# The first batch's attention cut into three query tiles, each followed by its LayerNorm and first MLP layer

## The chip, the cores and the metric

The kernel runs on one core of one Trainium2 chip. The metric is the device time of one execution in microseconds (us), from launch to the end of the last output write. The engines are TensorE (PE, matmuls; PEld are its weight loads), VectorE (DVE), ScalarE (ACT), GpSimd (POOL) and SyncE (SP), which here only starts DMAs. Each engine works through its own instructions in order and waits on semaphores for the others; ACT and POOL start some DMAs too.

## The reference

Eight batches of 12 heads, 448 tokens of 64 elements in each head; the heads' outputs side by side (768 columns) go through a LayerNorm and a two-layer MLP with 3072 hidden columns. All in float32 on input and output.

```
q_n = q / sqrt(mean(q*q) + 1e-6) * g_q ; k_n likewise with g_k       # over a head's 64 elements
P   = softmax(q_n @ k_n.T / 8) ; x = P @ v                           # [8, 12, 448, 64] -> [8, 448, 768]
xn  = (x - mean(x)) / sqrt(var(x) + 1e-6) * g_ln
out = x + relu(xn @ w_ch1) @ w_ch2                                   # w_ch1 [768, 3072], w_ch2 [3072, 768]
```

## The kernel before, in words

**Units.** Heads are taken in pairs, six pairs a batch, numbered p = 0 to 47 through all batches. A pair's 448 tokens lie as three full tiles of 128 and a left-over of 64 for each of the two heads, seven groups in all. Preparation works on units of two pairs (the first two units of batch 0 hold one pair each): squares on ACT (L218), sums on DVE (L221), a logarithm and an exponential on ACT for the inverse root (L224, L225), the keys times the product of the two gain vectors (L235, DVE or POOL), a high half of the keys in fp16 (L241 POOL or L243 ACT) and the remainder as a low half (L246, DVE), queries scaled and written twice (L68, L285). The keys' inverse root is not applied to the keys: it is the per-row scale of the exponential.

**Attention of a pair.** Seven key groups in turn: scores S (L359, a 128 x 448 matmul; the left-over groups L365 or L369 and L370), the exponential E (L377, ACT, 448 columns), and the product with v (V, L414 for three query tiles and L416 for the left-over, with a column of ones in v for the sum). L429 to L436 on DVE divide by the sums and write x. Keys and queries are transposed on PE through PSUM (L319, L322, L333, L336, copied out at L324, L339 and L341) up to unit 7, and by DMA transposes afterwards (L264 to L277).

**Order of the work.** For batch 0 the list ORDER gives, word by word, the program order of every step: letters a to m are preparation steps of a unit, K and Q transposes, S, V, T (LayerNorm statistics), A, N, X, R (the LayerNorm), U (`up_first`, the first 3 of 24 chunks of the first MLP layer), W0 to W2 (the weight loads of the first layer, 1024 columns each, issued on POOL) and L4 to L7 (unit loads, issued on SP). Every engine's queue follows this order. After it, `run_rest` interleaves two lists for each batch b: the MLP's chunks of batch b, and the attention steps of batch b+1, seven for each pair. `upto` keeps the steps in proportion to the chunks' costs, so that the steps are through when `tail` = 13 chunks of 960 cost units are left; then come the LayerNorm of batch b+1, four DMA transposes of its result on SP (L630), and these 13 chunks of the second layer (L674, psC) on PE beside it. The first layer's chunk is L658 (psH), six matmuls of 384 columns for an even batch (three token tiles) and 512 for an odd one, which also carries the left-over tokens of both; ACT applies the ReLU (L660).

**First loads.** `load_first` splits batch 0 over the ACT, SP and POOL queues pair by pair; SP's list ends with v. The second layer's weights (`load_w2`, two halves of 2304 KB) are started from the attention steps of units 6 and 7.

Of the kernel before, what the change touches and what calls it, by code (L numbers as in the profile page):

```python
# [32 lines left out]
z0 b2 a2 S0.2 d2 c2 S0.3 S0.4 K1 V0.0 e2 i2 S0.5 Q1 g2 l2 S0.6 S1.0 j2 V0.1 S1.1 S1.2 m2 b3  # L38
V0.2 a3 V0.3 k2 c3 S1.3 K2 V0.4 S1.4 z2 V0.5 Q2 S1.5 V0.6 V1.0 i3 W0 d3 e3 S1.6 V1.1 V1.2 S2.0
j3 T0 V1.3 S2.1 S2.2 Q3 V1.4 S2.3 K3 S2.4 V1.5 V1.6 S2.5 g3 z3 S2.6 V2.0 S3.0 S3.1 V2.1 k3  # L40
S3.2 b4 S3.3 V2.2 l3 a4 V2.3 m3 S3.4 V2.4 K4 S3.5 Q4 V2.5 V2.6 S3.6 Q5 S4.0 V3.0 S4.1 V3.1 i4
V3.2 d4 T1 K5 V3.3 W1 c4 V3.4 V3.5 S4.2 S4.3 V3.6 S4.4 S4.5 W2 e4 V4.0 V4.1 j4 S4.6 S5.0 k4
S5.1 g4 V4.2 l4 S5.2 V4.3 V4.4 V4.5 S5.3 K6 V4.6 z4 V5.0 S5.4 m4 b5 V5.1 G2 S5.5 L6 V5.2 S5.6
V5.3 V5.4 V5.5 Q6 a5 i5 V5.6 T3 T4 S6.0 S6.1 S6.2 S6.3 T5 S6.4 A V6.0 V6.1 N0 V6.2 N1 V6.3
S6.5 S6.6 d5 V6.4 X0 X1 U0 N2 R Q7 X2 c5 e5 j5 g5 k5 l5 z5 U1 U2 V6.5 M m5 V6.6 L7 K7
# [5 lines left out]
UP_FIRST = 3  # L51
# [25 lines left out]
class _Fast:  # L77


    def __init__(self, ctx, tc, sh, q, k, v, gs, g_ln, w1, w2, out):  # L80
# [57 lines left out]
    def load_first(self):  # L138
        nc = self.nc
        flat = self.hT.rearrange("p f n -> p (f n)").bitcast(FP32)  # L140
        t = [flat[:, 2688 * n:2688 * n + 2688].rearrange("p (w g d) -> p w g d", w=NPAIR, d=D)
             for n in range(2)]
        flat = self.sh.w2.rearrange("p f n -> p (f n)").bitcast(FP32)
        t.append(flat[:, 128:128 + 2688].rearrange("p (w g d) -> p w g d", w=NPAIR, d=D))
        main = lambda eng, n, p: self.load_main(eng, n, t[n][:, p, 0:6], 0, 2 * p, 2)
        left = lambda eng, n, p=0, m=NPAIR: self.load_left(eng, n, t[n][:, p:p + m, 6], 0, 2 * p, 2 * m)
        main(nc.scalar, 1, 0)
        left(nc.scalar, 1, 0, 1)
        main(nc.sync, 0, 0)
        left(nc.gpsimd, 0, 0, 1)  # L150
        main(nc.scalar, 0, 1)
        for n in range(2):
            nc.sync.dma_start(self.sh.gg[:, n], self.gs[n].unsqueeze(0))
        left(nc.gpsimd, 1, 1, NPAIR - 1)
        main(nc.sync, 1, 1)
        left(nc.sync, 0, 1, NPAIR - 1)
        for n, p in ((1, 2), (1, 3), (0, 2), (0, 3), (2, 0), (2, 1)):
            main(nc.sync, n, p)
        left(nc.sync, 2)
        for n, p in ((1, 4), (1, 5), (0, 4), (0, 5)):  # L160
            main(nc.sync, n, p)
        for p in range(2, NPAIR):
            main(nc.sync, 2, p)
        self.v_first = t[2]
        for u, (b, hs, m) in enumerate(UNITS):
            if b == 0:
                self.loads[u] = [x[:, hs // 2:hs // 2 + m].rearrange("p w g d -> p (w g) d")
                                 for x in t]
# [11 lines left out]
    def group(self, p, i):  # L180

        u, w = PAIR_UNIT[p]
        if UNITS[u][0] == 0:
            return 7 * w + i
        return 6 * w + i if i < 6 else 6 * UNITS[u][2] + w
# [6 lines left out]
    def pieces(self, u):  # L192
# [19 lines left out]
        def square(n):  # L212

            o = c["khl" if n == 1 else "qn"].rearrange("p g e d -> p (g e d)").bitcast(FP32)
            if u == 0 and n == 1:
                o = self.hT.rearrange("p f n -> p (f n)").bitcast(FP32)[:, 5376:5376 + g * D]
# [11 lines left out]
        def kg():  # L228
            if u == 0:
                nc.vector.tensor_tensor(out=sh.gprod[0:1], in0=sh.gg[:, 0], in1=sh.gg[:, 1],  # L230
                                        op=ALU.mult)
                ps = self.ps_m.tile([128, D], FP32, tag="mlp", name="psG")
                nc.tensor.matmul(ps, sh.row, sh.gprod[0:1], start=True, stop=True)
                nc.vector.tensor_copy(out=sh.gprod, in_=ps)
            (nc.vector if u in DVE_KG else nc.gpsimd).tensor_tensor(  # L235
                out=c["t"][1], in0=c["t"][1],
                in1=sh.gprod.unsqueeze(1).broadcast_to([128, g, D]), op=ALU.mult)
# [62 lines left out]

        def vall():

            nonlocal v16, vl, p1
            v16, vl, p1 = self.v16[:, 0:2], self.vl[:, 0:2], 2
            vmain()
            vleft()
# [4 lines left out]
                    z=vall if u == 0 else lambda: (vmain(), vleft()))  # L311


    def trans_k(self, p):
        nc, sh = self.nc, self.sh
        u, w = PAIR_UNIT[p]
        qn, khl = self.units[u][0:2]
        kT, ps = self.kU[PE_SET][:, 960 * (p % 2):960 * (p % 2) + 960], self.tr
        nc.tensor.matmul(ps[:, 0:256].rearrange("p (e o) -> p e o", e=2)[:, :, 0:D],  # L319
                         khl[:, self.group(p, 6)], sh.id16, is_transpose=True, start=True, stop=False)  # L320
        for i in range(6):
            nc.tensor.matmul(ps[:, 192 + 128 * i:320 + 128 * i], khl[:, self.group(p, i)], sh.id16,  # L322
                             is_transpose=True, start=False, stop=(i == 5))
        nc.vector.tensor_copy(out=kT, in_=ps[:, 0:960])  # L324

    def trans_q(self, p):
        nc, sh = self.nc, self.sh
        u, w = PAIR_UNIT[p]
        qn, khl = self.units[u][0:2]
        tr = self.ps_m.tile([128, 1024], FP16, tag="mlp", name="psQ") if p < NPAIR else self.tr  # L330
        ps = tr[:, 128:128 + 2 * S].rearrange("p (e s) -> p e s", e=2)
        qT = self.qU[PE_SET][:, p % 2].rearrange("p e s -> p (e s)")
# [5 lines left out]
        if p in ACT_Q:  # L338
            nc.scalar.copy(out=qT, in_=ps.rearrange("p e s -> p (e s)"))  # L339
# [106 lines left out]
    def first_attention(self):  # L446
# [531 lines left out]
```

## Time and profile before

| what | us |
|---|---|
| median of three runs | 603.84 (603.78 to 603.84) |
| span of the profiled execution, first to last instruction | 603.0 |
| PE busy | 577.6 |
| ACT busy | 358.5 |
| DVE busy | 287.8 |
| POOL busy | 184.8 |
| first exponential starts (timeline of ACT) | 12.08 |
| first 512-column first-layer matmul of batch 1 starts (timeline of PE) | 123.02 |

The profiled execution's span is 603.0 us; what lies around it up to the measured time of 603.84 us is 0.84 us, taken as fixed. A timeline row gives the start, the length, the engine, the line, what is written and read, the shape and how many instructions are merged; behind it, in brackets, stand the idle time before it and who ended it. A row of the stages' table gives, for a stretch of time, each engine's busy time with its instructions in brackets, then the granted TensorE clock, the busy share of the 16 DMA engines, and GB/s. Matmuls are pipelined: the length of one is longer than the distance to the next.

### The profile page before, as it was taken

How to read it: one execution, taken by the hardware profiler on the slowest of the kernel's cores; microseconds unless marked ns; L12 is line 12 of the kernel's file. 1: busy time of each engine (PE TensorE's matmuls, PEld its weight loads, DVE VectorE, ACT ScalarE, POOL GpSimd, SP SyncE). 2: the span in 40 equal slices, each digit the busy share in tenths (PEclk: the TensorE clock that was granted, in tenths of full speed). 3: DMA queues.
4: the chain of work that ended last, by engine and by line, in shares of the span. 5: the costliest groups of instructions: out<-in, count | busy, mean ns of one | idle time of the engine just before them, and what ended most of it. 6: DMA issues, size and time to landing. Idle time of an engine off the chain costs nothing.

```text
span 603.0 us, 11494 instructions
## 1 busy us (share of the span) xinstructions
PE 577.6 (96%) x4502; PEld 341.9 (57%) x4502; DVE 287.8 (48%) x645; ACT 358.5 (59%) x673; POOL 184.8 (31%) x246
## 2 busy tenths in 40 slices
PE   2877999999999999999999999999999999999997
PEld 1555566654566666655566666655556666654565
DVE  5798567734256255724256255642355422450011
ACT  5996887359743598548755498537765287114300
POOL 3844432232642345423542245505322000000000
PEclk9899999999999999999999999999999999999999
DMA  7999999574957578947866386848533330040011
GB/s 209 281 196 206 207 222 197 106 212 86 146 130 125 106 126 155 170 121 122 120 127 131 104 125 153 165 120 152 114 68 88 92 62 1 27 106 1 1 53 54
DMA packets 130285, 75.18 MB, mean 125 GB/s; under 512 B 96500, under 2 KB 120420, under 8 KB 130228
## 3 DMA queue, kind: packets, MB, share of 16 engines
q1 hardware_dynamic: 113092, 44.50, 37.7%
q0 software_dynamic: 16192, 29.30, 22.9%
q8 instruction: 36, 0.59, 0.4%
q10 hardware_dynamic: 944, 0.62, 0.3%
q14 instruction: 21, 0.17, 0.1%
HBM read 52.30 MB, written 11.01 MB: 105 GB/s over the span
## 4 chain that ended last, share of the span: by engine, by line
PE 88%; ACT 2%; DVE 2%; issue 0%; DVEq 0%
PE psC L674 36%; PE psH L658 35%; PE psS L359 8%; PE oA L414 5%; PE oB L416 2%; PE psS L365 1%; ACT E L377 1%; PE tr L322 0%; ACT khl L218 0%; PE psU L704 0%; DVE stat L582 0%; ACT hT L660 0%; PE tr L336 0%; DVE xn L603 0%; DVE x L431 0%
## 5 line engine op out<-in xcount | busy, mean ns | idle before, releaser
L658 PE MATMUL psH<-xnT,w 128*128 128x512 f16 (+1 forms) x1134 | 242.1, 353 | 0.0
L674 PE MATMUL psC<-w,hT 128*128 128x384 f16 (+1 forms) x1368 | 234.8, 324 | 0.0
L377 ACT ACTIVATE E<-psS,rr_all 128x448 f16<-128x448 f32 x312 | 193.5, 635 | 49.5 <-PE psS L359 48.6
L660 ACT ACTIVATE hT<-psH 128x512 f16<-128x512 f32 (+1 forms) x189 | 104.0, 550 | 130.9 <-PE psH L658 128.8
L674 PEld LDWEIGHTS <-hT 128*128 128x128 f16 x1368 | 127.2, 98 | 78.8 <-issue 4.3
L658 PEld LDWEIGHTS <-w 128*128 128x128 f16 x1134 | 102.3, 98 | 83.3 <-issue 2.9
L359 PE MATMUL psS<-qU,kU 128*128 128x448 f16 x288 | 101.3, 358 | 8.7 <-ACT E L377 5.8
L414 PEld LDWEIGHTS <-E 128*128 128x128 f16 x936 | 65.0, 99 | 44.3 <-issue 5.0
L235 POOL TENSOR_TENSOR qkv<-qkv,gprod 128x896 f32<-128x896 f32 x21 | 43.7, 2079 | 95.8 <-issue 51.7
L414 PE MATMUL oA<-v,E 128*128 128x65 f16 x864 | 66.9, 194 | 0.1
L678 DVE SCALAR_TENSOR_TENSOR x<-psC,rs_all,x 128x384 f32<-128x384 f32 x48 | 29.2, 616 | 78.4 <-PE psC L674 77.9
L128 POOL DMA_DIRECT2D qkv<-in_k_dram x14 | 11.1, 793 | 137.0 <-ACT E L377 64.3
L416 PE MATMUL oB<-v,E 128*128 128x65 f16 x288 | 52.1, 194 | 0.1
L429 DVE RECIPROCAL rec_all<-oA 128x6 f32<-128x6 f32 x48 | 9.3, 194 | 88.2 <-PE oA L414 87.8
L221 DVE TENSOR_REDUCE ssq<-khl 128x14 f32<-128x896 f32 (+1 forms) x24 | 25.6, 1065 | 44.6 <-ACT khl L218 44.5
L359 PEld LDWEIGHTS <-kU 128*128 128x128 f16 x288 | 28.2, 99 | 25.9 <-issue 6.0
L221 DVE TENSOR_REDUCE ssq<-qn 128x14 f32<-128x896 f32 (+1 forms) x25 | 26.2, 1046 | 21.8 <-ACT qn L218 21.7
L68 DVE SCALAR_TENSOR_TENSOR qn<-qkv,rr_all 128x256 f16<-128x256 f32 (+1 forms) x72 | 26.4, 426 | 18.1 <-ACT rr_all L225 18.1
L416 PEld LDWEIGHTS <-E 128*128 128x128 f16 x312 | 30.3, 97 | 0.2 <-DVE xl L436 0.2
L431 DVE TENSOR_TENSOR x<-oA,rec_all 128x384 f32<-128x384 f32 x48 | 26.8, 558 | 1.5
L582 DVE BATCH_NORM_STATS2 stat<-x 128x6 f32<-128x256 f32 (+1 forms) x75 | 26.0, 404 | 0.6
L246 DVE TENSOR_TENSOR khl<-qkv,khl 128x896 f16<-128x896 f32 x21 | 22.7, 1079 | 4.0 <-ACT khl L243 3.9
(114 smaller groups left out, 447.3 us busy)
## 6 DMA issues: line engine op xcount, KB each, us to landing
out_dram<-x SPq DMA_DIRECT2D x20, 384.0 KB, 2.5
qkv<-in_v_dram POOLq DMA_DIRECT2D x15, 384.0 KB, 6.5
qkv<-in_k_dram POOLq DMA_DIRECT2D x14, 384.0 KB, 3.9
qkv<-in_q_dram POOLq DMA_DIRECT2D x14, 384.0 KB, 5.4
w<-in_moe_w_ch_dram POOLq DMA_DIRECT2D x3, 1536.0 KB, 13.0
w<-in_moe_w_ch_dram POOLq DMA_DIRECT2D x2, 2304.0 KB, 24.8
qkv<-in_k_dram SPq DMA_DIRECT2D x7, 384.0 KB, 5.7
qkv<-in_q_dram SPq DMA_DIRECT2D x7, 384.0 KB, 6.0
```

What stands on the lines that cost most here:

```text
L68: nc.vector.scalar_tensor_tensor(out=out, in0=x, scalar=8.0, in1=r.unsqueeze(2).broadcast_to([x.shape[0], g, D]), op0=ALU.mult, op1=ALU.mult)
L221: nc.vector.tensor_reduce(out=c["ssq"][:, n], in_=c["sq", n], axis=AX.X, op=ALU.add)
L235: (nc.vector if u in DVE_KG else nc.gpsimd).tensor_tensor(out=c["t"][1], in0=c["t"][1], in1=sh.gprod.unsqueeze(1).broadcast_to([128, g, D] ...
L359: nc.tensor.matmul(ps[0][:, 0:S], c["main"][:, ts(i, 128)], c["q"][:, ts(h, S)], start=True, stop=True)
L377: nc.scalar.activation(out=o, in_=x[:, 0:S], func=AFT.Exp, scale=self.units[u][3][:, g:g + 1], bias=EXP_BIAS)
L414: nc.tensor.matmul(oA[:, t, cs], E[:, ts(t, 128)], rhs, start=(i == 0 and t == 0), stop=(i == 6 and t == 2))
L416: nc.tensor.matmul(oB[:, cs], E[:, 320:448], rhs, start=(i == 0), stop=(i == 6))
L431: nc.vector.tensor_tensor(out=x[:, :, 128 * hp:128 * hp + 128].rearrange("p t (e d) -> p t e d", e=2), in0=oA[:, :, :, 0:D], in1=rec[:, 0: ...
L658: nc.tensor.matmul(ps[:, 0:N], sh.w1[:, dc, ts(f, 128)], xnT[:, dc, 0:N], start=(dc == 0), stop=(dc == NDC - 1))
L660: nc.scalar.activation(out=hT[:, f, 0:N], in_=ps[:, 0:N], func=AFT.Relu)
L674: nc.tensor.matmul(ps[:, 0:g[1]], hT[:, f, ts(t, 128)], sh.w2[:, f, cols], start=(f == 0), stop=(f == NFF - 1))
L678: nc.vector.scalar_tensor_tensor(out=x[:, cols], in0=ps[:, 0:g[1]], scalar=self.rs[:, b, t:t + 1], in1=x[:, cols], op0=ALU.mult, op1=ALU.add)
```

## The change

Only batch 0 and the way into batch 1 change.

- Batch 0 runs in three phases: token tile 0, token tile 1, and token tile 2 with the left-over tokens. In each phase every pair's scores are taken for that phase's queries alone: 8 matmuls of 128 columns (phases 0 and 1), 9 pieces of 192, 128 or 64 columns (phase 2). The exponentials cover several key groups in one PSUM bank: 512 and 384 columns, in phase 2 512, 448 and 384.
- To allow this the keys are multiplied by their own inverse root in fp32 (L461) before they are split into halves, and the scale of the exponential is the constant 0.125. The gain vectors go into the queries, on POOL (L504). All six pairs' turned keys stay in SBUF.
- After each phase come that tile's division, LayerNorm (A, N, X, XC) and, for tiles 0 and 1, all 24 first-layer chunks in six groups of four (U, L641: 24 matmuls of 128 columns into one bank; R, L646: a ReLU of 512 columns). They stand between the scores of phases 1 and 2. Tile 2's six groups come from `mlp_chunks`, after ORDER.
- Loads: q and v of batch 0 go into the two buffers of the input ring, keys stay where they were. SP's list is reordered and ends with the left-over rows of q (`self.load_left(nc.sync, 0, ...)`, 196 KB in rows of 256 bytes). W0 stands in the order after the gain product of the second query part (qG0.2), W1 after z2 and j2, W2 after qG2.0; W3 and W4, the second layer's weights, are in ORDER too.
- The tail for batch 0 (that is, into batch 1) is TAIL0 = 8 chunks and no longer 13.

The diff, cut; `power` and `score` are new functions inside `first_pieces`:

```diff
-WARM = 22
-DVE_KG, POOL_HI, POOL_DUP, ACT_Q = (0, 1), (1, 2, 3, 4, 5), (1, 2, 4), (0, 1)
+POOL_HI, POOL_DUP = (0, 1, 2, 4, 5), (4,)
+KN_POOL, COPY_ACT, DUP_POOL = (1,), ('C4', 'QC2.4'), ('2.0', '0.2')
+Q_PARTS = ((0, 0, 2), (0, 2, 6), (1, 0, 6), (2, 0, 4), (2, 4, 6))
 ORDER = """
-b0 a0 c0 L4 i0 j0 e0 k0 gq0 l0 b1 m0 a1 c1 K0 Q0 d0 G gk0 S0.0 S0.1 d1 e1 L5 i1 g1 j1 l1 k1 m1
...
+spread a0 qa0.0 d0 a1 qG0.0 qt0.0 h0 d1 qg0.0 n0 h1 ql0.0 j0 qm0.0 n1 Q0.0 k0 QC0.0 K0 j1 C0
+qa0.2 k1 S0.0.0 a2 S0.0.1 qG0.2 qt0.2 K1 C1 E0.0.0 G W0 d2 qg0.2 S0.1.0 a3 z0 ql0.2 h2 d3
+E0.0.1 qm0.2 E0.1.0 S0.1.1 n2 z2 V0.0 Q0.2 h3 qa2.0 QC0.2 j2 n3 E0.1.1 W1 qa1.0 V0.1 k2 j3 z3
+qt1.0 K2 C2 qg1.0 qG1.0 L4 k3 K3 S0.2.0 S0.2.1 E0.2.0 C3 E0.2.1 qG2.0 ql1.0 K4 V0.2 C4 S0.3.0
+O0.0 S0.3.1 E0.3.1 K5 qm1.0 W2 T0.0 Q1.0 E0.3.0 C5 S0.4.0 G2 Q1.3 E0.4.0 QC1.0 S0.4.1 V0.3
+E0.4.1 QC1.3 S0.5.0 E0.5.0 S0.5.1 qt2.0 V0.4 E0.5.1 S1.0.0 E1.0.0 V0.5 S1.0.1 O0.1 E1.0.1
+S1.1.0 E1.1.0 S1.1.1 T0.1 V1.0 A0 E1.1.1 S1.2.0 N0 E1.2.0 S1.2.1 V1.1 X0 E1.2.1 S1.3.0 XC0
+qg2.0 V1.2 S1.3.1 O1.0 E1.3.0 U0.0 E1.3.1 ql2.0 qa2.4 V1.3 T1.0 S1.4.0 qm2.0 R0.0 S1.4.1 qt2.4
+U0.1 E1.4.1 qG2.4 qg2.4 Q2.0 E1.4.0 ql2.4 Q2.2 R0.1 V1.4 QC2.0 L5 S1.5.0 S1.5.1 QC2.2 E1.5.0
+U0.2 qm2.4 E1.5.1 V1.5 R0.2 S2.0.0 O1.1 Q2.4 E2.0.0 S2.0.1 U0.3 T1.1 QC2.4 A1 N1 E2.0.1 S2.0.2
+X1 R0.3 W3 S2.1.0 XC1 E2.1.0 U0.4 E2.0.2 S2.1.1 R0.4 U0.5 E2.1.1 S2.1.2 R0.5 S2.2.0 V2.0 E2.2.0
...
+V2.2 E2.4.1 U1.5 C7 L6 E2.3.2 O2.0 S2.4.2 R1.5 V2.3 E2.4.2 m4 S2.5.0 K6 T2.0 E2.5.0 S2.5.1 V2.4
+C6 E2.5.1 S2.5.2 Q6 E2.5.2 D6 V2.5 Q7 O2.1 S6.0 S6.1 S6.2 D7 S6.3 T2.1 S6.4 A2 N2 S6.5 X2 S6.6
+XC2 R M batch1
 """.split()
-UP_FIRST = 3
+TAIL0 = 8
 def load_first(self):
+        key(nc.scalar, 0)
+        self.load_left(nc.scalar, 1, tk[:, 0:1, 6], 0, 0, 2)
+        main(0, tq, 0, 2)
+        self.load_left(nc.gpsimd, 1, tk[:, 1:NPAIR, 6], 0, 2, 2 * NPAIR - 2)
+        key(nc.scalar, 1)
+        for n in range(2):
+            nc.sync.dma_start(self.sh.gg[:, n], self.gs[n].unsqueeze(0))
+        key(nc.sync, 2)
+        key(nc.sync, 3)
+        main(0, tq, 2, 4)
+        key(nc.sync, 4)
+        key(nc.sync, 5)
+        main(2, tv, 0, 2)
+        self.load_left(nc.sync, 2, tv[:, 36:42], 0, 0, H)
+        main(2, tv, 2, 4)
+        self.load_left(nc.sync, 0, tq[:, 36:42], 0, 0, H)
 def first_pieces(self):
+            def square():
+                start(c, g, "qn")
+                for y, a in zip(src, at):
+                    nc.scalar.activation(pair(c["sq"])[:, :, a], y, AFT.Square)
...
+        PARTS = {2: (((0, 0, 192), (1, 0, 192), (2, 0, 128)), ((2, 128, 192), (3, 0, 192), (4, 0, 192)),
+                     ((5, 0, 192), (6, 0, 192)))}
+        PARTS[0] = PARTS[1] = (tuple((i, 0, 128) for i in range(4)),
+                               tuple((i, 0, 128) for i in range(4, 7)))
...
+        def power(ph, p, k):
+            width = 192 if ph == 2 else 128
+            i, c0, _ = PARTS[ph][k][0]
+            a, n = width * i + c0, sum(c1 - c0 for _, c0, c1 in PARTS[ph][k])
+            nc.scalar.activation(out=E[ph, p][:, a:a + n], in_=psS[ph, p, k][:, 0:n], func=AFT.Exp,
+                                 scale=0.125, bias=EXP_BIAS)
...
+        def up(t, k):
+            ps = o["up", t, k] = self.ps_m.tile([128, 512], FP32, tag="mlp", name="psU")
+            for f in range(4):
+                for dc in range(NDC):
+                    nc.tensor.matmul(ps[:, ts(f, 128)], sh.w1[:, dc, ts(4 * k + f, 128)],
+                                     self.xnT[:, dc, ts(t, 128)],
+                                     start=(f == 0 and dc == 0), stop=(f == 3 and dc == NDC - 1))
 def mlp_chunks(self, b):
-        for f in range(0 if b else UP_FIRST, NFF):
+        for k in range(0 if b else 6):
+            if f"U2.{k}" not in ORDER:
+                yield 24 * 128 / 2.4, (lambda k=k: (self.ops[f"U2.{k}"](), self.ops[f"R2.{k}"]()))
+        for f in range(NFF if b else 0):
             yield 6 * N / 2.4, (lambda f=f: up(f))
 def run_rest(self):
-                upto(int(min(goal, start + (goal - start) * done / (total - 960 * tail))))
+                upto(int(min(goal, start + (goal - start) * done / (total - 960 * (tail if b else TAIL0)))))
```

A word such as S1.3.0 means scores of phase 1, pair 3, part 0; E, V, O, T likewise; qa, qt, qg, qG, ql, qm, Q and QC are a query part's square, sum, root, gain product, scaling, doubling, transposes and copy; h, n, j and k are a key unit's root, normalisation, high and low half; C copies turned keys out.

More of the change, by code (lines that the diff above doesn't have):

```diff
@@ L156, in load_first @@
[L156 to L168, printed above, removed]
+        key(nc.sync, 2)
@@ L228, in kg @@
         def kg():
[L229 to L235, printed above, removed]
+            nc.gpsimd.tensor_tensor(
                 out=c["t"][1], in0=c["t"][1],
@@ L505, in attention @@
                 pieces = pieces[:k]
-            if f"z{u}" in done and u == 4:
+            if f"z{u}" in done and f"m{u}" in done:
                 continue
```

399 lines of the change are left out of this document (271 added, 128 removed).

## The prediction

> **What bounds the kernel now.** I read the page first, then the table by stage, then the timelines around the point where batch 1's MLP begins. The page:
>
> ```profile
> span 603.0 us, 11494 instructions
> PE 577.6 (96%) x4502; PEld 341.9 (57%) x4502; DVE 287.8 (48%) x645; ACT 358.5 (59%) x673; POOL 184.8 (31%) x246
> PE   2877999999999999999999999999999999999997
> DMA  7999999574957578947866386848533330040011
> PE 88%; ACT 2%; DVE 2%; issue 0%; DVEq 0%
> ```
>
> PE is full from the fifth slice (60 us) on; there the time is columns through PE. Only the first 60 us have room, and in them the DMA engines are as full. The stages, cut where batch 0's values end (58.4), where batch 1's end (109.6), and where batch 1's first-layer matmuls begin (123.0):
>
> ```profile
> 0.00:12.00 12.00, 3.02 (x18) 2.18 (x19) 7.16 (x22) 5.63 (x12) 3.22 (x10) 1.00 0.72 198
> 12.00:26.00 14.00, 10.80 (x88) 6.84 (x87) 9.11 (x14) 12.55 (x23) 10.82 (x13) 0.88 0.96 274
> 26.00:58.40 32.40, 25.00 (x339) 17.60 (x336) 30.22 (x63) 26.79 (x53) 16.93 (x19) 1.00 1.06 222
> 58.40:109.60 51.20, 49.99 (x467) 32.41 (x465) 34.13 (x76) 41.79 (x80) 15.26 (x15) 1.00 1.11 192
> 109.60:123.00 13.40, 13.33 (x83) 7.86 (x83) 10.13 (x21) 2.67 (x6) 3.85 (x5) 1.00 0.61 162
> ```
>
> From 12 to 58.4 PE idles 46.4 - 35.8 = 10.6 us; DVE (30.2 of 32.4) and ACT (12.6 of 14, then 26.8) hold it. Busy time flatters PE, as its ends are modelled: by the code 63,300 columns pass in these 58.4 us, 27.7 us at the 56 ns for 128 of step 3, so 31 us are empty, 12 of them before the first exponential. At most 19 us can be won by filling waits with first-layer matmuls: 584. The DMA column stands at 0.96 and 1.06.
>
> **How I sum.** Before and after, 210,500 columns pass PE ahead of batch 1's first 512-column matmul, and the instructions behind it are the same. So I follow the changed kernel to that point and compare with 123.02.
>
> **Step 1, the loads (a wait that is new).** Rows: the SP queue alone (16 to 20), beside a weight load with 256-byte rows (30 to 35) and with 768-byte rows (47 to 54), and landings of single issues.
>
> ```profile
> q1 hardware_dynamic: 1980, 1.30, 107.9%
> qkv<-in_v_dram SPq DMA_DIRECT2D x1, 32.0 KB, 4.1
> ...
> q0 software_dynamic: 452, 0.93, 98.0%
> q1 hardware_dynamic: 332, 0.11, 13.7%
> ...
> q0 software_dynamic: 567, 1.16, 87.3%
> q1 hardware_dynamic: 537, 0.40, 23.0%
> ...
> w<-in_moe_w_ch_dram POOLq DMA_DIRECT2D x1, 1536.0 KB, 12.7
> ...
> w<-in_moe_w_ch_dram POOLq DMA_DIRECT2D x2, 1536.0 KB, 17.1
> ...
> qkv<-in_v_dram SPq DMA_DIRECT2D x1, 32.0 KB, 9.3
> ...
> w<-in_moe_w_ch_dram POOLq DMA_DIRECT2D x2, 2304.0 KB, 24.8
> ```
>
> Alone, SP's queue moves 1.30 MB in 4 us, 326 GB/s. Beside a weight load (q0, POOL's) the packets go about one for one, 567 to 537, and since a weight packet is 2048 bytes, SP gets 0.40 MB in 7 us (57 GB/s), and 22 GB/s with 256-byte packets. A left-over v load landed after 9.3 us beside a weight load, after 4.1 without. W0, issued at 25.9, landed 12.7 us later at 38.6; the next two, issued at 36.2 on average, land 17.1 us later in the mean, 53.3 = 38.6 + 1.5 d, so d = 9.8 us for each, and about 3 us pass before the first data.
>
> In the changed order W0 waits on POOL for little: q pairs 2 to 5 are in when 2.16 MB are (0:12 moved 198 GB/s, so 11 us), the square and the gain product take 0.55 and 1.2 us by columns from these rows, so W0 is issued at about 13 and flows from 16.
>
> ```profile
> L218 ACT ACTIVATE khl<-hT 128x896 f32<-128x896 f32 x2 | 1.9, 936 | 0.0
> L235 POOL TENSOR_TENSOR hT<-hT,gprod 128x896 f32<-128x896 f32 x2 | 4.2, 2076 | 0.2
> 12.08 1.16 ACT L377 ACTIVATE E<-psS,rr_all 128x448 f16<-128x448 f32 x2 [0.33 <-PE psS L359]
> 37.22 4.04 ACT L377 ACTIVATE E<-psS,rr_all 128x448 f16<-128x448 f32 x7
> ```
>
> By 16 us 2.38 + 4 x 0.3 = 3.6 of batch 0's 4.13 MB are in. What is last on SP, the rest of v and the 196 KB of q's left-over rows, meets W0. The left rows need 768 packets, W0 has 768: they land when W0 does, at about 26. **Who waits:** the square qa2.0 on ACT. Behind it, in order, stand the exponential E0.1.1, the squares of phase 1, the high half j3, and on PE V0.1 and then K2. On POOL z2 waits for v, and j2 and W1 behind it. The first exponential itself comes at about 13 (before: 12.08). Unmeasured is only how much of the left rows W0 overtakes: none (landing 17.5) to all and the rest of v too (28). I take 26, the nearer to the 9.3 us row.
>
> **Step 2, to the first new MLP group U0.0.** After the landing ACT does a rest square, E0.1.1, qa1.0 and j3 (0.3 + 0.5 + 0.8 + 0.9), DVE the sum, copy C2 and low half k3 behind them, then S0.2.0: 5.5 us, 31.5. Then 15 exponentials to E1.3.0: seven in the row above take 0.57 us each for 448 columns, so 0.62 and 0.52 for 512 and 384: 8.6 us with C4 (0.9) and a root (0.45), 10 us; DVE has as much in the stretch (two low halves, copies, two divisions, one LayerNorm), so 10.5. The width of the exponentials wins nothing: 42 before and after, 18,816 columns. U0.0 at **42**.
>
> **Step 3, U0.0 to the last values of batch 0.** 61,700 columns: 12 groups U (36,864), scores, values and transposes. ACT has 22 us beside it (23 exponentials at 0.57, 12 ReLUs of 0.5, two squares and a copy), so PE sets the pace. Weight loads are tripled; the row that bears on it:
>
> ```profile
> 55.65 2.17 PE L704 MATMUL psU<-xnT,w 128*128 128x128 f16 x36
> L708 ACT ACTIVATE hT<-psU 128x384 f16<-128x384 f32 x3 | 1.2, 482 | 0.0
> ...
> L658 PEld LDWEIGHTS <-w 128*128 128x128 f16 x1134 | 102.3, 98 | 83.3 <-issue 2.9
> ```
>
> 36 matmuls of 128 columns, each with its own weights, in 2.17 us less the last one's tail of 0.2: 56 ns each, the column rate, although a weight load is 98 ns long: they overlap, and I cost nothing. 26.9 + 0.5 = 27.3 us: **69.3**. W1 and W2 (9.8 us each behind W0) are in by 48, before U0.4 at 51.
>
> The Trainium skill, "TensorE: Matmul & The Clock Gate", section "Back-to-back issue gap", speaks against the change: in a stream of weight load and matmul pairs it measured about 81 ns a matmul at 128 columns. By that the 432 in U would cost 25 ns more each, 10.8 us; the trace's 56 ns disagrees.
>
> **Step 4, tile 2's LayerNorm.** Nothing but 1.5 us of batch 1's scores covers it: divisions (1.5), a copy (0.6), statistics (0.45), 0.2, normalisation (1.0), transposes and copy (1.0).
>
> ```profile
> L431 DVE TENSOR_TENSOR x<-oA,rec_all 128x384 f32<-128x384 f32 x7 | 3.9, 558 | 0.2
> L603 DVE SCALAR_TENSOR_TENSOR xn<-x,stat,gln 128x768 f16<-128x768 f32 x2 | 2.0, 1012 | 0.0
> L645 DVE COPY xnT<-tr 128x768 f16<-128x768 f16 x1 | 0.6, 558 | 0.6 <-PE tr L637 0.6
> ```
>
> 4.8 us: **74.1**.
>
> **Step 5, batch 1's attention.** 99,100 columns (before 115,500 in 51.2 us, row 58.4:109.6; same rate): 43.9 us. The same preparation, about 39 us of ACT and 40 of DVE, now has 44 us instead of 51. **118.0**.
>
> **Step 6, the shorter tail.** Before, the values end at 109.57; then
>
> ```profile
> 109.57 0.83 PE L365 MATMUL psS<-qU,kU 128*64 128x448 f16 x4
> 110.33 12.85 PE L674 MATMUL psC<-w,hT 128*128 128x384 f16 x78
> 113.25 2.93 DVE L603 SCALAR_TENSOR_TENSOR xn<-x,stat,gln 128x768 f16<-128x768 f32 x3
> 114.38 5.21 SPq L630 DMA_TRANSPOSE xnT<-xn  x4
> 123.02 1.24 PE L658 MATMUL psH<-xnT,w 128*128 128x512 f16 x5
> ```
>
> The last DMA transpose is issued by 119.6 - 1.3 = 118.3 and needs about 2.8 us to land (the same step's first: issue 114.38): 11.6 us after the values. 78 matmuls covered it with 1.8 us over. After, 48 remain: 0.8 + 7.8 = 8.6 us, so PE waits 3: 118.0 + 11.9 = **129.9**.
>
> Sum: 129.9 - 123.0 = +6.9; 603.0 + 6.9 = 609.9, and with the 0.84 us outside the span **610.7 us**. Costed at nothing: the gain product on POOL for the queries (POOL 31% busy; were it bare, 6 us), the normalised keys (it takes the old product's place, one for one), fewer `least` and memsets (0.6 us, off the path), W3 and W4 (24.8 us each in the last row above: in by 73 and 98, needed where the columns reach the second layer's halves, at about 86 and 107; a later one would cost its lateness).
>
> **The rivals.**
> - *The weights set it, not the left rows.* SP's queue is through before W0 flows. U0.0 comes at 32.5, but U0.4 waits for W2, 16 + 3 x 9.8 = 45.4; from 46 on 40,700 columns take 17.7 us: 64.2 instead of 69.3, **605.6**. For it: 16:20 ran at 326 GB/s. Against: the left rows are last.
> - *Faster.* PE's waits are really filled: W2 lands early enough that U0.4 starts before 43.5, and batch 1 runs at the pure column rate (12.85 us for 78 matmuls of 384, 0.163 each: 42.0 us, 2 less). Then 605.6 - 2.5 - 2 - 1 = **600** (584 at the very most). Decided at U0.4: before 43.5 it is faster. For it: 31 us without columns. Against: DMA share 1.06, since W2 cannot land before its bytes have passed.
> - *ACT and DVE become the bound in batch 1.* 40 us of DVE at 0.85 busy is 47.5 us: **614**.
> - *The weight loads no longer hide* in the long groups of 128 columns (against it: 36 in a row at 56 ns). At a load's 98 ns each, 432 x 42 ns is 18 us: **629**. The rule of "Back-to-back issue gap" in the Trainium skill, cited at step 3, would give 621.
>
> **How the numbers follow.** Forecast 43% (610.7; alone 607 to 614), weights 25%, faster 21%, batch-1 bound 8%, weight loads 3%. The range from 600 to 616 leaves out about half of the faster case and the upper ends, 2 in 10. A measurement of this kernel tells 0.2% (1.2 us) from no change. Faster 0.22 (the faster case and the weights' low end), same 0.08 (between the two), slower 0.70.
>
> **What would show it.** Step 1: idle ACT before L500 or L596 between 18 and 26, ended by the DMA of q's left rows; POOL's z2 late. Step 2: U0.0 at 42. Step 3: PE without gaps from there; 56 ns in L641. A wait of PE for W2 before U0.4 is the second case. Step 6: an idle PE of about 3 us before L878. The prediction is wrong if left rows land by 18 and W2 by 43, or if the DMA transposes are issued earlier relative to the values.

## The result and the profile after

| | before | changed |
|---|---|---|
| median, us (runs) | 603.81 (4) | 620.88 (4) |
| range | 603.54 to 603.84 | 620.43 to 621.66 |
| span of the profiled execution | 603.0 | 619.5 |
| batch 1's first 512-column matmul | 123.02 | 139.36 |

The ratio is 1.0281, 95% interval 1.0266 to 1.0295: 17.1 us slower, where 6.9 were forecast (610.7, range 600 to 616). The page of the changed kernel: span, PE's busy time, its slices, the granted clock, the DMA slices, and the chain by engine.

```profile
span 619.5 us, 12191 instructions
PE 580.2 (94%) x4856; PEld 358.7 (58%) x4856; DVE 296.5 (48%) x634; ACT 356.5 (58%) x675; POOL 190.6 (31%) x250
...
PE   2499869979999999999999999999999999999997
...
PEclk9999989999999999999999999999999999999999
DMA  8999963358398468796367489666453420040011
...
PE 83%; DVE 8%; ACT 2%; DMA 2%; issue 2%; POOL 1%; SPq 0%; DVEq 0%; ACTq 0%; POOLq 0%
```

PE is full from the third slice on, two earlier than before, and then has holes that it did not have: the sixth slice (77 to 93 us) stands at 6 in PE and at 8 in the row of the granted clock. DVE's share of the chain went from 2% to 8%. The same kernel cut where the new first-layer groups begin (39.4), where batch 0's values end (67.4), where tile 2's first-layer group begins (72.75), at 90, and where batch 1's values end; the columns are PE, PEld, DVE, ACT, POOL, granted clock, DMA share, GB/s.

```profile
0.00:12.00 12.00, 1.80 (x12) 1.38 (x13) 6.58 (x20) 3.97 (x11) 5.32 (x12) 1.00 0.82 246
12.00:39.40 27.40, 17.54 (x208) 14.75 (x207) 24.13 (x31) 17.14 (x37) 19.39 (x19) 1.00 1.10 230
39.40:67.40 28.00, 27.55 (x510) 27.17 (x508) 15.63 (x29) 21.54 (x45) 10.08 (x11) 1.00 1.22 220
67.40:72.75 5.35, 3.21 (x21) 1.42 (x21) 4.55 (x12) 3.54 (x7) 0.00 (x0) 1.00 1.24 223
72.75:90.00 17.25, 12.40 (x183) 11.37 (x183) 13.12 (x17) 11.59 (x23) 9.46 (x9) 0.91 0.74 151
90.00:127.05 37.05, 33.65 (x360) 22.62 (x357) 26.22 (x57) 26.32 (x46) 6.74 (x8) 1.00 0.41 108
127.05:139.40 12.35, 8.64 (x54) 4.94 (x54) 10.11 (x21) 3.29 (x7) 4.84 (x5) 1.00 0.61 140
```

The granted clock of 1.00 in the first two rows is not a reading: the clock records of this trace begin at 32.2 us (before: at 18.3). Up to there PE's 128-column matmuls stand 106 ns apart, behind it 55; in the kernel before they are 106 ns apart up to 18.3 us and again from 21.7 to 25.1. Six transposes of 128 columns on either side of that point, in the changed kernel:

```profile
31.31 0.85 PE L293 MATMUL tr<-id,khl 128*128 128x128 f16 x6
...
38.28 0.51 PE L864 MATMUL tr<-id,xn 128*128 128x128 f16 x6 [0.37 <-DVE xn L832]
```

**A ledger of empty time.** Counted from the matmul records, 210,560 columns pass PE ahead of the first 512-column matmul in both kernels, 87.7 us at 2.4 columns a ns. What is left of a stretch after its columns I call empty: waits, gaps and time at a lower clock together.

| stretch | before: length, columns, empty | changed: length, columns, empty | added |
|---|---|---|---|
| start and batch 0 (to 58.4; to 72.75) | 58.4, 26.55, 31.9 | 72.75, 38.0, 34.75 | 2.9 |
| batch 1's attention (to 109.6; to 127.06) | 51.2, 48.3, 2.9 | 54.3, 41.7, 12.6 | 9.7 |
| tail (to 123.02; to 139.36) | 13.4, 12.85, 0.5 | 12.3, 8.05, 4.3 | 3.7 |

Together 16.3 us. The filling worked: 27,500 more columns passed in the first stretch for 2.9 us of added empty time. At half rate 5.3 us of columns passed in the changed kernel's first stretch and 5.0 us in the one before, and each takes as long again, so the clock is about 5 us of the empty time of either and only 0.3 of the 2.9. The largest loss is in batch 1's attention. Its timeline, several engines:

```profile
78.74 0.94 ACT L207 ACTIVATE khl<-qkv 128x896 f32<-128x896 f32 x1
78.83 0.83 POOL L270 CAST v<-qkv 128x768 f16<-128x768 f32 x1
78.92 1.68 DVE L229 TENSOR_TENSOR khl<-qkv,khl 128x896 f16<-128x896 f32 x1 [1.08 <-POOL khl L224]
79.58 0.94 ACT L207 ACTIVATE qn<-qkv 128x896 f32<-128x896 f32 x1
79.76 2.78 POOL L218 TENSOR_TENSOR qkv<-qkv,gprod 128x896 f32<-128x896 f32 x1
80.42 0.62 ACT L351 ACTIVATE E<-psS,rr_all 128x448 f16<-128x448 f32 x1
80.52 2.97 DVE L71 SCALAR_TENSOR_TENSOR qn<-qkv,rr_all 128x896 f16<-128x896 f32 x1
...
81.09 0.35 PE L333 MATMUL psS<-qU,kU 128*128 128x448 f16 x1 [2.19 <-ACT E L351]
...
83.41 1.07 DVE L210 TENSOR_REDUCE ssq<-khl 128x14 f32<-128x896 f32 x1
...
84.57 0.95 ACT L226 ACTIVATE khl<-qkv 128x896 f16<-128x896 f32 x1 [2.52 <-DVE ssq L210]
...
86.10 0.35 PE L333 MATMUL psS<-qU,kU 128*128 128x448 f16 x1 [2.49 <-ACT E L351]
...
88.04 2.54 PE L641 MATMUL psU<-xnT,w 128*128 128x128 f16 x24
```

Read it backwards from PE's two waits. The first (2.19) is for an exponential that stood on ACT behind unit 6's two squares. The second (2.49): ACT's cast at 84.57 overwrites the tile that holds unit 6's squares, so it waits for DVE's sum at 83.41, which stood behind unit 5's query division, which took 2.97 us instead of 1.08. Behind the cast wait the exponentials, and behind them PE. Then a group of 24 matmuls takes 2.54 us instead of 1.50: the granted clock, at 1.00 until then, fell.

```profile
80.00:86.00 6.00, 2.51 (x41) 2.23 (x41) 6.00 (x5) 3.48 (x7) 5.43 (x6) 1.00 0.19 30
86.00:90.00 4.00, 3.74 (x36) 3.27 (x36) 3.66 (x8) 2.55 (x7) 0.00 (x0) 0.60 0.76 218
```

4 us at 0.60 are 1.6 us lost, paid on top of the hole. Both preparations stand here because unit 5's, which the order before held among batch 0's last steps, now begins after tile 2's first group, and unit 6's follows at once (EARLY: steps 42 to 49 and 47 to 56).

**Theories.** (A) The two preparations side by side make the loss. (B) *Thin fill*: batch 1's attention lost 16,000 columns of first-layer work, and its exponentials and preparations are now the pace wherever they stand. (C) For the rest, the bare spots of my own sum: the tail, tile 2's LayerNorm, the left-over rows.

### The profile page after: what moved, and what is told of

It reads as the page before. It is cut to its first block, busy times and chain, and to the rows that moved or that the text cites. A ratio compares the mean times of both kernels' runs of the same rounds, so it can differ in the third digit from the quotient of the medians.

```text
span 619.5 us, 12191 instructions
## 1 busy us (share of the span) xinstructions
PE 580.2 (94%) x4856; PEld 358.7 (58%) x4856; DVE 296.5 (48%) x634; ACT 356.5 (58%) x675; POOL 190.6 (31%) x250
## 3 DMA queue, kind: packets, MB, share of 16 engines
q1 hardware_dynamic: 113092, 44.53, 36.9%
## 4 chain that ended last, share of the span: by engine, by line
PE 83%; DVE 8%; ACT 2%; DMA 2%; issue 2%; POOL 1%; SPq 0%; DVEq 0%; ACTq 0%; POOLq 0%
PE psC L894 32%; PE psH L878 31%; PE psS L333 7%; PE oA L384 4%; PE psU L641 3%; PE oB L386 2%; PE psS L339 1%; DVE ssq L210 1%; ACT khl L207 1%; DMA xnT<-xn 1%; DVE xn L832 1%; DVE qn L71 1%; PE psS L585 1%; DVE khl L471 1%; DMA qkv<-in_v_dram 1%
## 5 line engine op out<-in xcount | busy, mean ns | idle before, releaser
L878 PE MATMUL psH<-xnT,w 128*128 128x512 f16 (+1 forms) x1008 | 218.4, 356 | 3.0 <-DMA xnT<-xn 3.0
L351 ACT ACTIVATE E<-psS,rr_all 128x448 f16<-128x448 f32 x273 | 170.9, 636 | 54.3 <-PE psS L333 52.6
L880 ACT ACTIVATE hT<-psH 128x512 f16<-128x512 f32 (+1 forms) x168 | 93.7, 558 | 121.9 <-PE psH L878 120.3
L878 PEld LDWEIGHTS <-w 128*128 128x128 f16 x1008 | 90.7, 98 | 79.2 <-issue 5.5
L333 PE MATMUL psS<-qU,kU 128*128 128x448 f16 x252 | 87.6, 353 | 8.7 <-ACT E L351 8.1
L384 PEld LDWEIGHTS <-E 128*128 128x128 f16 x819 | 57.2, 98 | 44.4 <-issue 6.2
L898 DVE SCALAR_TENSOR_TENSOR x<-psC,rs_all,x 128x384 f32<-128x384 f32 x48 | 29.3, 616 | 76.1 <-PE psC L894 75.7
L384 PE MATMUL oA<-v,E 128*128 128x65 f16 x756 | 59.4, 194 | 0.4 <-DVE x L401 0.3
L210 DVE TENSOR_REDUCE ssq<-khl 128x14 f32<-128x896 f32 x21 | 22.8, 1084 | 51.0 <-ACT khl L207 51.0
L210 DVE TENSOR_REDUCE ssq<-qn 128x14 f32<-128x896 f32 x21 | 22.8, 1084 | 24.4 <-ACT qn L207 24.3
L641 PE MATMUL psU<-xnT,w 128*128 128x128 f16 x432 | 27.8, 223 | 0.3 <-DVE xnT L674 0.3
L386 PEld LDWEIGHTS <-E 128*128 128x128 f16 x273 | 26.4, 97 | 0.6 <-DVE xl L406 0.5
L641 PEld LDWEIGHTS <-w 128*128 128x128 f16 x432 | 26.1, 100 | 0.8 <-issue 0.5
```

Source lines behind the costliest of these rows:

```text
L210: nc.vector.tensor_reduce(out=c["ssq"][:, n], in_=c["sq", n], axis=AX.X, op=ALU.add)
L333: nc.tensor.matmul(ps[0][:, 0:S], c["main"][:, ts(i, 128)], c["q"][:, ts(h, S)], start=True, stop=True)
L351: nc.scalar.activation(out=o, in_=x[:, 0:S], func=AFT.Exp, scale=self.units[u][3][:, g:g + 1], bias=EXP_BIAS)
L384: nc.tensor.matmul(oA[:, t, cs], E[:, ts(t, 128)], rhs, start=(i == 0 and t == 0), stop=(i == 6 and t == 2))
L386: nc.tensor.matmul(oB[:, cs], E[:, 320:448], rhs, start=(i == 0), stop=(i == 6))
L641: nc.tensor.matmul(ps[:, ts(f, 128)], sh.w1[:, dc, ts(4 * k + f, 128)], self.xnT[:, dc, ts(t, 128)], start=(f == 0 and dc == 0), stop=(f = ...
```

## The experiments

Each was timed in 3 rounds beside the kernel before. Behind the first 512-column matmul all kernels hold the same instructions, which took 479.7 to 481.4 us in the profiled executions, so the start of that matmul is a sharper measure than the time (the upper end is five runs in which the clock stands at half rate for up to 3.4 us right behind it); "attention" is the stretch from tile 2's first group to batch 1's last values, with its columns and its empty time.

| run | median | ratio, 95% interval | attention: columns, empty | first 512 columns |
|---|---|---|---|---|
| changed, again | 621.49 | 1.0279, 1.0251 to 1.0307 | 41.7, 11.4 | 138.64 |
| 13 chunks kept back | 619.81 | 1.0270, 1.0246 to 1.0294 | 36.9, 14.0 | 136.93 |
| unit 6 later | 618.99 | 1.0257, 1.0236 to 1.0278 | 41.7, 8.8 | 135.42 |
| unit 5 earlier | 616.62 | 1.0224, 1.0198 to 1.0251 | 41.7, 7.5 | 134.27 |
| first MLP of tiles 0 and 1 behind | 629.20 | 1.0418, 1.0398 to 1.0438 | (stretch differs) | 146.36 |
| cover for tile 2's LayerNorm | 621.15 | 1.0280, 1.0253 to 1.0308 | 41.7, 12.7 | 139.12 |
| high half first | 621.04 | 1.0285, 1.0245 to 1.0326 | 41.7, 13.6 | 139.64 |
| unit 5 earlier, 6 and 7 spread | 616.05 | 1.0184, 1.0139 to 1.0229 | 41.7, 6.4 | 133.78 |
| unit 5 earlier, 13 chunks | 614.55 | 1.0182, 1.0164 to 1.0200 | 36.9, 10.0 | 133.08 |
| four edits together | 614.26 | 1.0171, 1.0148 to 1.0194 | 36.9, 8.4 | 132.08 |
| unit 5 earlier, 2 chunks | 619.73 | 1.0261, 1.0238 to 1.0284 | 47.4, 4.1 | 136.61 |
| weights later | 622.43 | 1.0319, 1.0285 to 1.0354 | 41.7, 12.9 | 140.46 |

The changed kernel run again is the measure for the rest:

> The changed kernel itself, once more, as the measure for the runs beside it: 620.9 us (620 to 622) by every theory.

It came as expected. In its profile the half clock fell at 82 to 86 us (0.59) instead of 86 to 90, the first 512-column matmul came 0.7 us earlier and the attention had 1.2 us less empty time. One profile of a kernel is no sharper than that.

**Unit 6 later.**

```diff
-EARLY = {5: (42, 49), 6: (47, 56), ...
+EARLY = {5: (42, 49), 6: (55, 62), ...
```

> Unit 6's preparation starts 8 attention steps later, so that it no longer stands beside unit 5's; PE's order is the same. Theory, two preparations side by side: from 75 to 90 us PE fell 7.3 us behind its columns (before: 0.9), as exponentials stood on ACT behind squares and a cast that waited for DVE's sums, and DVE's 1.08 us division took 2.97 us beside POOL's product. With the units apart about two thirds of that goes: 616 us (614 to 618), and the stretch from 80 to 90 has PE at 8 of 10 us or more. Rival, thin fill: ACT has as much to do as before over the same columns and PE's waits only move to where unit 6 now stands: 620 to 622.

A row of DVE's timeline and the stages of this run:

```profile
80.47 1.17 DVE L71 SCALAR_TENSOR_TENSOR qn<-qkv,rr_all 128x896 f16<-128x896 f32 x1
```

```profile
72.70:90.00 17.30, 14.57 (x228) 12.57 (x228) 10.29 (x18) 13.10 (x25) 8.77 (x7) 1.00 0.81 174
90.00:123.10 33.10, 29.96 (x318) 19.85 (x314) 27.02 (x57) 24.25 (x45) 7.43 (x10) 1.00 0.41 109
```

With unit 6's product gone from POOL the same division takes 1.17 us, the clock stays at 1.00, and the first 512-column matmul comes 3.9 us earlier (3.2 against the changed kernel's second profile). The median shows 1.9 to 2.5 us of it, and its interval overlaps the changed kernel's; theory A's 5 us was too much, and by the matmul's start B's nothing was too little.

**Unit 5 earlier.**

```diff
-C6 E2.5.1 S2.5.2 Q6 E2.5.2 D6 V2.5 Q7 O2.1 S6.0 S6.1 S6.2 D7 S6.3 T2.1 S6.4 A2 N2 S6.5 X2 S6.6
-XC2 R M batch1
+C6 E2.5.1 S2.5.2 Q6 E2.5.2 b5 a5 i5 D6 V2.5 Q7 O2.1 S6.0 S6.1 S6.2 D7 S6.3 T2.1 S6.4 z5 A2 N2 S6.5
+X2 c5 S6.6 XC2 R d5 j5 e5 M g5 k5 l5 m5 L7 batch1
...
-                if c:
+                if c or p == nb0:
```

> Unit 5's preparation is spread over the end of batch 0 (squares before and among batch 1's first scores, the gain product on POOL beside tile 2's LayerNorm); PE's order is the same. Theory, two preparations side by side: 4 to 6 us less than the changed kernel, 615 to 617, with a small part given back as tile 2's LayerNorm on DVE runs beside POOL. Rival, thin fill: no gain, 620 to 622, or slower by the 1 to 2 us for which the squares hold the exponentials at 66 us.

```profile
75.22 1.09 DVE L229 TENSOR_TENSOR khl<-qkv,khl 128x896 f16<-128x896 f32 x1
76.23 1.08 DVE L71 SCALAR_TENSOR_TENSOR qn<-qkv,rr_all 128x896 f16<-128x896 f32 x1
```

```profile
72.87:90.00 17.13, 15.13 (x232) 12.99 (x232) 12.52 (x22) 13.43 (x27) 5.28 (x5) 1.00 1.01 228
90.00:122.00 32.00, 29.13 (x310) 19.44 (x308) 24.34 (x52) 22.75 (x40) 6.75 (x8) 1.00 0.31 83
```

4.3 to 4.9 us less, as theory A had it, with the same matmuls in the same order: the division takes 1.08 us, the clock stays at 1.00, and of 12.6 us of empty time 5.2 go (4.0 of the second profile's 11.4). Tile 2's LayerNorm gave nothing back (tile 2's first group at 72.87). But 7.5 us stay, where the kernel before has 2.9: A is not the whole.

**13 chunks kept back** (TAIL0 = 8 becomes 13).

> Only the number of second-layer chunks kept back behind batch 1's attention changes, 8 to 13. Theory of the tail: the 3.0 us for which PE waits for batch 1's transposes before its first 512-column matmul go, since 30 more matmuls of 384 columns (4.9 us) stand in the gap, and nothing else changes: 617.9 us, 3.0 less than the changed kernel's 620.9. Rival, thin fill: these 4.8 us of columns are taken from between batch 1's scores and values, where PE already waits for exponentials; PE then waits there for as much as it wins at the end: 620 to 622.

The wait for the transposes is gone, and new waits stand in the attention, the largest 3.56 us; a row of PE's timeline:

```profile
80.36 0.53 PE L333 MATMUL psS<-qU,kU 128*128 128x448 f16 x1 [3.56 <-ACT E L351]
```

4.8 us of columns left the attention, and it got only 3.4 us shorter (2.2 against the second profile). By the medians about half of the 3 us came out at the end: 1.1 to 1.7. The intervals overlap, so the time alone does not tell this.

**The first MLP of tiles 0 and 1 behind batch 0** (U0, R0, U1, R1 taken out of the order):

```diff
-        for k in range(0 if b else 6):
-            if f"U2.{k}" not in ORDER:
+        for k in [f"{t}.{k}" for t in range(0 if b else 3) for k in range(6)]:
+            if f"U{k}" not in ORDER:
```

> The first MLP of query tiles 0 and 1 (288 matmuls of 128 columns, 15.4 us of columns) goes back behind batch 0, in the same pieces as tile 2's; the rest of the change stays. Theory, the early first layer pays where it stands and the loss behind it is the two preparations side by side: batch 0's second half loses its cover, as in the kernel before (8 us of waits from 40 to 60), and the collision of the two preparations stays on ACT and DVE: 621 to 625. Rival, thin fill: batch 1's attention has its columns back and runs at the rate of the kernel before, about 51 us plus 8 for the extra columns, behind batch 0's values at about 57: 612 to 617.

629.2 us, slower than either theory had it. The stage from 39.4 to batch 0's last values:

```profile
39.40:66.50 27.10, 19.04 (x234) 16.08 (x231) 16.01 (x30) 15.71 (x33) 10.09 (x11) 0.69 1.19 212
```

276 matmuls fewer than in the changed kernel's stage (234 against 510), and it is only 1 us shorter, at a granted clock of 0.69. So the early first layer is worth 8 us where it stands, and part of that is the clock, which a thinly used PE did not keep. The strong form of B, that filling batch 0 only moves the waits, falls.

**Cover for tile 2's LayerNorm** (U1.4, R1.4, U1.5 and R1.5 moved behind V2.5, among S6.1 to S6.4).

> Two of query tile 1's first-layer groups (2.56 us of columns) are taken out of the stretch before batch 0's last values, where PE was full, and stand among batch 1's first scores, where PE waited from 67.4 to 72.75 us for exponentials and for tile 2's LayerNorm. Theory, that LayerNorm chain is bare (PE fell 2.7 us behind its columns there): 2 to 2.5 us less than the changed kernel, PE 7 of 8 us busy from 67 to 75. Rival, ACT and not PE sets the stretch before: the last values come no earlier for it, and the time stays: 620 to 622.

```profile
60.80 0.35 PE L585 MATMUL psS<-qU,kU 128*128 128x64 f16 x3 [0.75 <-ACT E L596]
...
65.65 0.22 PE L307 MATMUL tr<-id,qn 128*128 128x128 f16 x1 [1.26 <-DVE kU L300]
```

The rival holds: with the two groups gone PE waits for ACT and DVE in the stretch before. Tile 2's first group comes 33.4 us behind the first new group, in the changed kernel 33.3, and the time stays.

**High half first** (j2 ahead of z2 on POOL).

> On POOL alone the cast of the third key unit's high half stands ahead of the values' casts instead of behind them. Theory, the start is set by POOL in order and by DVE's slower two-input operations beside POOL: PE waited 2.99 us for that unit's low half at 24.54; the low half comes about 1 us earlier, and since everything from there on follows in order, the first new first-layer group comes 1 us earlier and so does the end: 620 us, 1 less. Rival, q's left-over rows set it (the square behind them on ACT, as I forecast in step 1): no change, 620.9.

PE's timeline and the stages:

```profile
22.75 0.29 PE L290 MATMUL tr<-id,khl 128*128 128x128 f16 x1 [2.47 <-DVE khl L471]
...
38.43 1.50 PE L641 MATMUL psU<-xnT,w 128*128 128x128 f16 x24
```

```profile
66.00:70.00 4.00, 2.68 (x22) 1.12 (x18) 3.80 (x9) 2.61 (x5) 0.00 (x0) 1.00 1.24 221
70.00:74.00 4.00, 3.44 (x31) 2.87 (x31) 1.43 (x5) 1.63 (x5) 0.00 (x0) 0.57 1.23 228
```

The third unit's transposes come earlier: at 22.75 us, where they come at 23.7 to 24.5 with this order unchanged. The first new group comes 1.0 us earlier than in the changed kernel's profile, but this is not shown to be the edit's work. In nine profiled executions with the start unchanged it came at 38.68 to 39.99, in the main the later, the longer PE's first half rate lasted (to between 31.5 and 34.2 us, here to 29.3), and with the same edit in "four edits together" it came at 39.44. The time stays, as the rival had it, but its reason, the left-over rows, does not hold by "weights later" below. In this profile the clock also fell to 0.57 behind the hole of tile 2's LayerNorm (1.7 us).

**Unit 5 earlier, units 6 and 7 spread** (EARLY 6: (48, 61), 7: (62, 75)).

> Unit 5 earlier, as in the run that moved it alone (616.6 us), and the preparations of units 6 and 7 stretched over 13 attention steps instead of 9 and 8; PE's order is the same. Theory, what is left of the loss in batch 1 is bursts: while a unit is prepared, ACT has an exponential and a square or a cast to each step and PE waits 0.5 to 0.9 us for it, five times between 79 and 114: 614 to 615. Rival, thin fill: ACT's sum per column is what counts, however it is spread: 616 to 617.

616.05, at the lower edge of the rival's range. Empty time fell by 1.1 us to 6.4, and this run had the half clock at 72 to 76 (0.62), of which 0.8 us fall into the attention. Its runs lie 5 us apart; by the profile the bursts are 1 to 2 us of what is left.

**The sum of both losses (unit 5 earlier, 13 chunks), and four edits together.**

> Unit 5 earlier (alone 616.6 us; first 512-column matmul at 134.3 us) and 13 chunks kept back instead of 8 (alone 619.8 us; 136.9 against 139.4 us). Theory, the two losses are separate: 134.3 less 2.4, so the first 512-column matmul at about 132 and 614 us. Rival, thin fill: with the units apart the taken columns are missed between the scores, and PE waits there for what it wins: 134 and 616 to 617 us.

> Unit 5 earlier, units 6 and 7 stretched over 13 steps, 13 chunks kept back, and the cast of the third key unit's high half ahead of the values' casts. If the losses are separate: first 512-column matmul at 133.8 less 2.4 less 1 for the start, 130.4, and 612 to 613 us; if PE's half clock comes behind the hole at 67 to 72 us, as it did in two of the profiled runs, 1.7 us more. No theory has it below the kernel before, 603.8: the 5 us of the start and the 2 to 3 us of tile 2's LayerNorm stay.

614.55 and 614.26. With two edits the time is that of separate losses (614), but the first 512-column matmul comes at 133.1, midway between separate losses (132) and thin fill (134): with 13 chunks kept back the attention is empty for 10.0 us instead of 7.5. Four edits miss their forecast of 612 to 613 us and 130.4; the matmul comes at 132.1. The two kernels do not differ by more than their runs do. They are the fastest here, 6 to 7 us better than the changed kernel and about 11 behind the kernel before, which none of these edits reached.

**Unit 5 earlier, 2 chunks kept back.** This asks for the rest directly: more columns in the same attention.

> Unit 5 earlier and only 2 chunks kept back instead of 8, so that 5.8 us more of second-layer columns stand between batch 1's scores and values. What counts is how much PE waits from tile 2's first-layer groups to batch 1's last values: 11.0 us with 13 chunks kept back, 8.4 with 8. Thin fill: it goes on falling, to about 5 to 6, the last values come 3 us later than with 8 (at about 125 instead of 121.8), and the end 3 us later, 619 to 620, as the 12.5 us from there to the first 512-column matmul are set by the transposes. Rival, what is left are bursts of preparation that wait for DVE and ACT in order, whatever the fill: 8 us stay, the last values at 127.5, the end at 622.

```profile
73.34:90.00 16.66, 16.03 (x235) 13.58 (x235) 12.03 (x21) 12.61 (x26) 4.32 (x5) 1.00 0.98 227
90.00:124.90 34.90, 33.79 (x343) 22.23 (x341) 26.02 (x55) 24.19 (x43) 6.92 (x9) 1.00 0.36 96
124.90:136.60 11.70, 2.75 (x17) 1.29 (x17) 9.08 (x19) 2.64 (x6) 4.87 (x5) 0.71 0.68 159
```

As thin fill had it, the last values come at 124.9 and the end at 619.7. PE is full from 73 to 125, and the waits return in the tail, with a lower clock (0.71). Empty time by columns in the attention, all with unit 5 earlier: 10.0 us at 36.9, 7.5 at 41.7, 4.1 at 47.4 (the expectations give 11.0 and 8.4 for the first two, a count that ran from the gaps and not from the columns). Each us of columns taken away shortens the stretch by only 0.4 to 0.5 us. The kernel before, 48.3 and 2.9, lies near the same line. That is theory B, for what A leaves. The three points are single profiles. With 8 chunks kept back PE's listed waits in the attention are 4.9 us, 3.8 of them for exponentials, while ACT is busy 74% of it (36.2 of 49.1 us). So most of these waits are for exponentials on an ACT that is not full; what delays them there was not tested, beyond the spreading.

**Weights later** (W0 behind z2).

> The changed kernel with the first weight load issued behind the values' casts, some 6 us later, so that q's left-over rows have the queues for themselves. My forecast's step 1, the weight load holds these rows and with them ACT and PE: they land by 17.5 us and the first new first-layer group comes 2 us earlier or more. Rival, read from the trace after: ACT waited 0.47 us for these rows, POOL's and DVE's casts set PE's wait there; the first group comes at 39.4 within 0.6, and later the third weight load, some 5 us later too, makes PE wait 2 to 3 us: 621 to 624.

```profile
39.66 1.50 PE L641 MATMUL psU<-xnT,w 128*128 128x128 f16 x24
...
50.10 1.51 PE L641 MATMUL psU<-xnT,w 128*128 128x128 f16 x24 [0.44 <-DMA w<-in_moe_w_ch_dram]
```

The first new group comes no earlier, so the weight load did not hold it up, although ACT now takes the square of these rows without a wait. The third weight load made PE wait 0.44 us, not 2 to 3, and the time, 622.4 us, lies in the rival's range.

## Why the prediction failed, step by step

**Step 1, the loads: wrong mechanism, small effect.** W0 was issued when I said (13.94 against 13), but the left rows did not land with it at 26. Rows of ACT, POOL and PE in the changed kernel:

```profile
13.94 0.88 POOL L785 DMA_DIRECT2D w<-in_moe_w_ch_dram  x1
...
20.30 0.42 ACT L500 ACTIVATE qn<-qkv 128x256 f32<-128x256 f32 x1 [0.47 <-DMA qkv<-in_q_dram]
...
24.54 0.29 PE L290 MATMUL tr<-id,khl 128*128 128x128 f16 x1 [2.99 <-DVE khl L471]
```

ACT waited 0.47 us for them, until 20.30. The rows went ahead of the weights: from 15 to 17 us SP's queue passed 1004 packets, the weight load's 33. PE's wait of 2.99 was for the third key unit's low half, behind POOL's casts.

**Step 2, first new group at 42: it came at 39.44**, 2.6 us early. What the trace shows in place of step 1's wait to 26 is the landing by 20.3 and PE's 2.99 us behind POOL's casts. That the error is only 2.6 us is luck: the rows came 5.7 us earlier than I had them, and the stretch behind them took 19.1 us where I summed 16. I had no term for PE's half rate, which lasts to 32.2 us here, and the 31 us that I called empty in the kernel before hold 5.0 us of it.

**Step 3: right.** Batch 0's last values end at 67.4, 27.9 us on (27.3 forecast); the rows:

```profile
39.44 1.50 PE L641 MATMUL psU<-xnT,w 128*128 128x128 f16 x24
...
49.27 1.50 PE L641 MATMUL psU<-xnT,w 128*128 128x128 f16 x24
...
72.75 4.18 PE L641 MATMUL psU<-xnT,w 128*128 128x128 f16 x72 [0.27 <-DVE xnT L674]
```

24 matmuls with their own weights in 1.50 us less a tail of 0.2: 56 ns each again, and U0.4 at 49.27 waits for no weights.

**Step 4, 4.8 us for tile 2's LayerNorm: 5.4.** With the steps before, tile 2's first group stands at 72.75 against 74.1: up to here I was 1.35 us too slow.

**Step 5, batch 1's attention in 43.9 us: this is the step that failed.** It took 54.3 (100,032 columns, as forecast within 1%). "Same rate" was the error. About 5.2 us (4.0 by the second profile) are two preparations side by side, undone by moving unit 5 alone; I wrote that the same preparation stood in the stretch, when the diff had moved one unit more into it, directly ahead of the next. In that sum 1.6 us are the clock. The other 5 or so are thin fill: the rate of a stretch in which PE is full, with ACT 82% and DVE 67% busy beside it, does not hold when PE's columns are taken out. Spreading units 6 and 7 took back 1 to 2 us of them. My busy sums were near, 39 of ACT and 40 of DVE against 37.9 and 39.3. My own rival had the right name, ACT and DVE become the bound, but at 8% and with a price from DVE at 0.85 busy (614): DVE stood at 0.72, and a busy share knows nothing of waits in order.

**Step 6, the tail: right.** Forecast 11.9 us with a wait of 3; the timeline of the changed kernel:

```profile
126.83 0.22 PE L386 MATMUL oB<-vl,EL 128*128 128x130 f16 x1
...
128.41 7.97 PE L894 MATMUL psC<-w,hT 128*128 128x384 f16 x48
...
132.45 5.21 SPq L860 DMA_TRANSPOSE xnT<-xn  x4
...
139.36 1.46 PE L878 MATMUL psH<-xnT,w 128*128 128x512 f16 x6 [2.98 <-DMA xnT<-xn]
```

12.3 us, 2.98 of them waiting. The sum of the errors is 10.4 - 1.35 + 0.4 = 9.4 us, from 129.9 to 139.36. Of the rivals, "weights" needed the first group at 32.5 and a wait at U0.4, "faster" U0.4 before 43.5; it came at 49.27 without a wait, so neither was met. "Weight loads no longer hide" fell with step 3.

Not settled is why the start and batch 0 have 2.9 us more empty time than before. By columns the clock is 0.3 of it. I tried two causes there (weights, the high half), and neither is shown to move the first group or the end. What a full clock from the start would win, no run here shows.

## What to carry to other kernels

Work moved to fill an early hole is taken from a later stretch: price that stretch again from its own waits, with the list of what every engine must do in it, and never by the rate that it had while it was full. Follow each preparation that the diff drops from an order to the place where it now stands, and look what stands beside it there. And count a hole in PE's work twice where the profile's clock row dips behind holes; look at the distance of PE's matmuls too, since the row says nothing ahead of the trace's first clock record.

## What the runs showed of the hardware that was not expected

- **DVE's operations with two inputs in SBUF waited for POOL's operation to end.** In the changed kernel POOL's product ends at 79.76 + 2.78 = 82.54, DVE's division beside it at 80.52 + 2.97 = 83.49, 0.95 us later, about its own 1.08; POOL's cast ends at 79.66, DVE's subtraction at 80.60, 0.94 later. The sum at 83.41, with one input, took its 1.07 beside POOL. The Trainium skill, "SBUF — State Buffer", section "Who interferes with whom", states this: a VectorE instruction with two SBUF inputs contends with a GpSimd instruction that reads SBUF, and the port pair that they share is an exclusive lock. The trace agrees.
- **The clock falls behind short holes.** In the changed kernel waits of 2.2 and 2.5 us within 7 us were followed by 4 us at 0.60. In the changed kernel run again the clock stood at 0.59 from 82 to 86 us, and in "high half first" at 0.57 from 70 to 74, behind the hole of tile 2's LayerNorm. Each was worth 1.6 to 1.7 us. In the six runs with the units apart no wait between 76 and 90 us passed 1.6 us, and the clock stayed at 1.00 there. The traces record the clock in windows of 3.41 us, each at full or at half rate. Counted by columns over these windows up to 160 us, in all 14 traces, the clock fell behind windows that were filled to 13 to 34% (once 38%) and stayed full behind windows filled to 36% or more; at half rate it came back behind windows filled to 81% or more and stayed down up to 71%. The Trainium skill, "TensorE: Matmul & The Clock Gate", section "What's actually happening", gives windows of about 3.4 us that run freely and a half rate after an idle one. Its section "HAM oscillation — how this bites in real kernels" puts the limit at idle gaps of over about 3.4 us. The length of the dips and their moving place agree. The limit does not: in the changed kernel no gap between 76 and 87 us was over 2.5 us, 41 matmuls ran from 80 to 86, and the clock fell all the same.
